# One product's weight tiles moved by 64 bytes within a 512-byte period of SBUF, in an attention and low-rank MLP kernel

## The chip, the cores and the metric

One NeuronCore of a Trainium2 chip runs the whole program. The metric is the device time of one execution in microseconds. A profiled execution has a time of its own, and a span: first to last recorded instruction.

## The reference, cut to what matters

```python
# q, k, v: (8, 8, 576, 64); omega: (128, 64)
q_p, k_p = phi(q * scale), phi(k * scale)     # exp(x @ omega.T - |x|^2/2 - max) / sqrt(128)
attn = (q_p @ (k_p.T @ v)) / (q_p @ k_p.sum(axis=2) + 1e-6)
x = attn.transpose(0, 2, 1, 3).reshape(8, 576, 512)
u = x + (x.transpose(0, 2, 1) @ U @ V).transpose(0, 2, 1)
out = u + np.maximum(u @ w_ch1, 0.0) @ w_ch2  # w_ch1: 512 x 2048, w_ch2: 2048 x 512
```

Inputs and output are float32 (the MLP's weights are decoded from 64-bit words). 4608 rows go through the MLP.

## The kernel before

The work has three stages in order of time. The attention with the mixing by `U` and `V` takes the first 323 us. Then `u @ w_ch1` and the ReLU run until about 690 us, and the product with `w_ch2` runs to the end. The change touches the second and the third stage.

The 4608 rows are cut into 9 chunks `c` of 512 rows, the 2048 columns of `w_ch1` into 4 groups `g` of 512. A block product is done as seven half-size products (Strassen-like sums, `PRODUCTS = 7`), numbered `i`. A float32 number is split into a high and a low part of type float32r, so every product is made of three matmuls: high by high, low by high, high by low.

**Second stage, `unit(c, g, ...)`.** For each of the seven products there are 2 x 2 x 3 = 12 matmuls in L996. Each loads 128 x 128 of a weight tile (`wh` or `wl`, the operand that is held) and streams 256 columns of the right side's tile (`uh` or `ul`, the operand that moves):

```python
for x, y in ((wh, uh), (wl, uh), (wh, ul)):
    K(nc.tensor.matmul(p[:, f, :], x[:, k, fs], y[:, k, :], ...))
```

A chunk from chunk 2 on is 4 groups x 7 products x 12 = 336 matmuls. The order on TensorE is the order of the program (`K` keeps it).

**Third stage, L1379.** 36 steps `n` of 7 products of 12 matmuls. Here the weights of `w_ch2` are the operand that moves, and the left side (`gh`, `gl`; in step 0 also `uT`, `uraw` and `gs`) is held. The weights of group 0 are used in the even steps alone, 6 matmuls for each product.

**Where the weights lie.** `w_slot(g, i)` gives the pair `wh`, `wl` of group `g` and product `i`, 2048 bytes each in a partition. Groups 0 and 1 are in pool `wa`, which is filled from low addresses upward. Groups 2 and 3 are in pool `wb` at the other end. The third stage calls `w_slot` again, so the `w_ch2` tiles take the same places. Several pads in the kernel (`shift`, `rim`) set where the pools start. In the built program the addresses modulo 512 bytes are these:

| tiles | bytes modulo 512 |
|---|---|
| all `wh`, `wl` of groups 0 to 3 | 448 |
| `uh`, `ul` (right side of chunks 0 and 2 to 8) | 128 |
| right side of chunk 1 (it lies in the `wh3`, `wl3` places) | 448 |
| `gh`, `gl`, `gs` (left side of the third stage) | 256 |
| `uT`, `uraw` (left side of the first products of step 0) | 448 |

So moving address less held address, in 64-byte lines modulo 8, is (128 - 448)/64 = 3 for nearly all of the second stage, (448 - 256)/64 = 3 for nearly all of the third, and 0 for chunk 1 and the start of step 0. This text calls it the distance.

Chunks 0 and 1 are interleaved by groups at first, which ends at about 413 us. Chunk 2 runs from there to 452.4 us, and the six chunks 3 to 8 from 452.4 to 689.8 us.

Of the kernel before, what the change touches and what calls it, by code (L numbers as in the profile page):

```python
# [9 lines left out]
F32 = mybir.dt.float32  # L10
F32R = mybir.dt.float32r
# [18 lines left out]
def performer_mlp_kernel(ctx: ExitStack, tc, q, k, v, omega, U, V, w1, w2, out):  # L30
# [12 lines left out]
    P = 128  # L43
# [36 lines left out]
    wpools = {g: wa for g in range(EARLY_GROUPS)}  # L80
# [137 lines left out]

    def w_slot(g, i):
        i = (i - 2) % 7 if g == NG - 1 else i  # L220
        return [wpools[g].tile([P, 2, 2 * P], F32R, name=f"w{a}{g}_{i}") for a in "hl"]

    def operand(g, i):
        if (g, i) not in wops:
            if g == NG - 1 and i < 2:
                if not spares:
                    room = late["rx"].tile([P, 2, PIECE, 2], U32, name="graw0").bitcast(F32R)
                    spares.extend(room.rearrange("p s (k t) w -> p (s k) (t w)", k=2)[:, j] for j in range(4))
                wops[g, i] = [x.rearrange("p (k t) -> p k t", k=2) for x in spares[2 * i : 2 * i + 2]]
            else:  # L230
                wops[g, i] = w_slot(g, i)
        return wops[g, i]
# [823 lines left out]
    def w_place(g):  # L1056
        return lambda i: w_slot(g, i)
# [5 lines left out]
    tp = aside.enter_context(tc.tile_pool(name="tp", bufs=1))  # L1063
    guest_raws = loads(1, tp)
    guest = prepare(1, next(guest_raws), place=lambda i: w_slot(NG - 1, i + 2), lows=(VE, G_) * 3 + (VE,), pool=tp)
    for n, _ in enumerate(mixers[0]):
        if n == 2:
# [166 lines left out]
    for n in range(2, len(order)):  # L1234
        c, g = order[n]
# [123 lines left out]
    for n in range(NS):  # L1359
# [9 lines left out]
        for i in range(PRODUCTS):  # L1369
# [4 lines left out]
            for k in range(4):  # L1374
                g, f = divmod(now.s * 4 + k, 2)
# [70 lines left out]
```

## Time and profile before

| | |
|---|---|
| three runs | 1042.4, 1042.58 and 1048.74 us, median 1042.58 us |
| the profiled execution | 1039.76 us, span 1037.9 us |
| granted TensorE clock, mean over the span | 0.99 |
| TensorE busy, matmul and weight load | 1016.7 and 994.7 us |
| VectorE, ScalarE, GpSimd busy | 849.3, 612.7 and 518.2 us |

A matmul's record begins when the matmul starts and lasts some 0.28 us, though the next one starts after about 0.11 to 0.12 us: records overlap. The pace of the engine is thus read from the distance between starts (the spacing), or from the number of matmuls in a stretch. A stretch counts every matmul that overlaps it, so the spacing is (length + 0.28 us) / count.

### The profile page before, as it was taken

How to read it: one execution, taken by the hardware profiler on the slowest of the kernel's cores; microseconds unless marked ns; L12 is line 12 of the kernel's file. 1: busy time of each engine (PE TensorE's matmuls, PEld its weight loads, DVE VectorE, ACT ScalarE, POOL GpSimd, SP SyncE). 2: the span in 40 equal slices, each digit the busy share in tenths (PEclk: the TensorE clock that was granted, in tenths of full speed). 3: DMA queues.
4: the chain of work that ended last, by engine and by line, in shares of the span. 5: the costliest groups of instructions: out<-in, count | busy, mean ns of one | idle time of the engine just before them, and what ended most of it. 6: DMA issues, size and time to landing. Idle time of an engine off the chain costs nothing.

```text
span 1037.9 us, 23872 instructions
## 1 busy us (share of the span) xinstructions
PE 1016.7 (98%) x8497; PEld 994.7 (96%) x8497; DVE 849.3 (82%) x1510; ACT 612.7 (59%) x1479; POOL 518.2 (50%) x453
## 2 busy tenths in 40 slices
PE   8999999999999989999999999999999999999998
PEld 7998999989988889999999999999999999999998
DVE  4798898998898787666557665779999999999995
ACT  5889899989874556545364453763534444444442
POOL 3446967776433543323405214446575755646543
PEclk9899999999998999999999999999999999999999
DMA  7788687685435775987678767874545555455451
GB/s 136 138 159 155 139 194 142 128 193 121 95 82 126 208 186 123 238 240 193 183 190 222 196 176 246 243 218 158 184 172 183 174 162 176 161 178 178 135 182 51
DMA packets 380630, 175.51 MB, mean 169 GB/s; under 512 B 275680, under 2 KB 353504, under 8 KB 376032
## 3 DMA queue, kind: packets, MB, share of 16 engines
q1 hardware_dynamic: 378144, 173.70, 63.5%
q8 instruction: 67, 1.10, 0.4%
q10 hardware_dynamic: 2368, 0.30, 0.2%
q14 instruction: 51, 0.42, 0.1%
HBM read 109.97 MB, written 63.96 MB: 168 GB/s over the span
## 4 chain that ended last, share of the span: by engine, by line
PE 55%; DVE 2%; DMA 1%; issue 1%; ACT 1%; POOL 0%; SPq 0%; DVEq 0%; ACTq 0%
PE p_p L1379 9%; PE p_q L1379 8%; PE p_n L1379 7%; PE p_n L996 7%; PE p_q L996 5%; PE p_p L996 5%; PE p_kv L1379 4%; PE p_kv L996 3%; PE p_m L996 3%; PE p_m L1379 2%; DMA raw<-in_moe_w_ch_dram 1%; DVE g L984 1%; DMA graw<-g 1%; DVE gl L1224 0%; DMA g<-g 0%
## 5 line engine op out<-in xcount | busy, mean ns | idle before, releaser
L770 ACT ACTIVATE e<-p_p,nm 128x128 f32<-128x128 f32 x576 | 166.1, 397 | 23.3 <-DVE nm L763 16.3
L1217 ACT CAST gh<-gs 128x512 fp32r<-128x512 f32 x140 | 86.4, 622 | 153.0 <-DVE gs L1189 93.1
L1189 POOL TENSOR_TENSOR gs<-graw 128x512 f32<-128x512 f32 x70 | 113.6, 1634 | 121.3 <-DMA graw<-g 86.3
L980 ACT ACTIVATE g<-g 128x512 f32<-128x512 f32 x105 | 66.4, 632 | 165.0 <-DVE g L984 100.7
L636 POOL TENSOR_TENSOR xl<-xT,xh 128x384 fp32r<-128x384 f32 x96 | 97.4, 1031 | 97.5 <-ACT xh L632 80.4
L1224 DVE TENSOR_TENSOR gl<-gs,gh 128x512 fp32r<-128x512 f32 x140 | 137.7, 990 | 6.8 <-ACT gh L1217 6.0
L763 DVE TENSOR_REDUCE nm<-p_p 128x4 f32<-128x512 f32 x144 | 98.1, 683 | 27.0 <-PE p_p L757 12.1
L183 POOL TENSOR_TENSOR wf<-wf,low 128x512 int32<-128x512 int32 (+2 forms) x35 | 43.9, 1254 | 139.9 <-ACT g L980 76.7
L755 PE MATMUL p_p<-omh,xh 128*128 128x256 f32 x288 | 93.5, 325 | 3.6 <-ACT e L770 2.6
L1304 POOL TENSOR_TENSOR u<-u,p 128x256 f32<-128x256 f32 x72 | 80.8, 1151 | 25.7 <-DVE u L1304 23.2
L1224 DVE TENSOR_TENSOR gl<-graw,gh 128x512 fp32r<-128x512 f32 x107 | 84.3, 812 | 4.0 <-ACT gh L1217 4.0
L757 PE MATMUL p_p<-omh,xl 128*128 128x256 f32 x288 | 81.7, 284 | 0.6 <-POOL xl L636 0.6
L756 PE MATMUL p_p<-oml,xh 128*128 128x256 f32 x288 | 81.6, 283 | 0.0
L1379 PE MATMUL p_p<-wh,gh 128*128 128x256 f32 x288 | 79.5, 276 | 0.0
L1379 PE MATMUL p_p<-wl,gh 128*128 128x256 f32 x288 | 79.5, 276 | 0.0
L1379 PE MATMUL p_p<-wh,gl 128*128 128x256 f32 x288 | 79.5, 276 | 0.0
L1217 ACT CAST gh<-graw 128x512 fp32r<-128x512 f32 x107 | 63.4, 619 | 25.9 <-PE p_n L1379 5.1
L1379 PE MATMUL p_q<-wh,gl 128*128 128x256 f32 x276 | 76.3, 276 | 0.0
L1379 PE MATMUL p_q<-wh,gh 128*128 128x256 f32 x276 | 76.2, 276 | 0.0
L1379 PE MATMUL p_q<-wl,gh 128*128 128x256 f32 x276 | 76.2, 276 | 0.0
L713 PE MATMUL p_n<-kv,eT 128*128 128x65 f32 x512 | 73.6, 274 | 1.9 <-ACT eT L698 1.1
L713 PEld LDWEIGHTS p_n<-kv,eT 128*128 128x128 f32 x512 | 68.8, 196 | 5.1 <-ACT eT L698 1.4
(271 smaller groups left out, 3984.0 us busy)
## 6 DMA issues: line engine op xcount, KB each, us to landing
g<-g SPq DMA_DIRECT2D x282, 128.0 KB, 2.3
graw<-g SPq DMA_DIRECT2D x35, 1024.0 KB, 5.2
raw<-in_moe_w_ch_dram SPq DMA_DIRECT2D x22, 512.0 KB, 4.7
u_dram<-ut SPq DMA_DIRECT2D x36, 256.0 KB, 2.5
u<-u_dram SPq DMA_DIRECT2D x36, 256.0 KB, 2.6
out_dram<-u SPq DMA_DIRECT2D x36, 256.0 KB, 2.2
kt<-in_k_dram SPq DMA_DIRECT2D x120, 72.0 KB, 2.5
qt<-in_q_dram SPq DMA_DIRECT2D x120, 72.0 KB, 2.5
```

The lines of the kernel that those rows point to most:

```text
L636: nc.gpsimd.tensor_tensor(out=self.xl[-1], in0=self.turned, in1=f32(self.xh[-1]), op=ALU.subtract)
L713: nc.tensor.matmul(pn[:, h, :], eT[:, h, :], kv[:, h, s // 5, :], start=True, stop=True)
L755: nc.tensor.matmul(o, part.xh[g][:, ts], oh, start=True, stop=False)
L756: nc.tensor.matmul(o, part.xh[g][:, ts], ol, start=False, stop=False)
L757: nc.tensor.matmul(o, part.xl[g][:, ts], oh, start=False, stop=True)
L763: nc.vector.tensor_reduce(out=self.nm[:, :n], in_=self.pp[:, :n], axis=AX.X, op=ALU.max, negate=True)
L770: nc.scalar.activation(out=self.e[:, j, :], in_=self.pp[:, j, :], func=AF.Exp, bias=self.nm[:, j : j + 1])
L996: K(nc.tensor.matmul(p[:, f, :], x[:, k, fs], y[:, k, :], start=first, stop=(k == 1 and y is ul), skip_group_check=True,))
L1189: K(engine.tensor_tensor(out=to, in0=self.val[x], in1=self.val[y], op=op))
L1217: K(nc.scalar.copy(out=h, in_=v))
L1224: K(nc.vector.tensor_tensor(out=l, in0=v, in1=f32(h), op=ALU.subtract))
L1379: K(nc.tensor.matmul(acc[bank][:, half, :], x[:, ks], y[:, f, :], start=(now.s == 0 and k == 0 and half == 0 and x is h and y is wh), stop ...
```

## The change

`w_slot` takes, for group 0 and product 1 alone, a pad of 112 floats (448 bytes) ahead of the two tiles and one of 16 floats (64 bytes) behind them.

```diff
     def w_slot(g, i):
         i = (i - 2) % 7 if g == NG - 1 else i
-        return [wpools[g].tile([P, 2, 2 * P], F32R, name=f"w{a}{g}_{i}") for a in "hl"]
+        pool = wpools[g]
+        if (g, i) == (0, 1):
+            pool.tile([P, 112], F32, name="before")
+        tiles = [pool.tile([P, 2, 2 * P], F32R, name=f"w{a}{g}_{i}") for a in "hl"]
+        if (g, i) == (0, 1):
+            pool.tile([P, 16], F32, name="behind")
+        return tiles
```

No instruction reads or writes the pads. The instructions of the built program and their order and waits are the same on every engine. The addresses are not: the two tiles go from 20928 and 22976 to 21376 and 23424, which is 384 modulo 512. Everything that was above them at that end of SBUF goes up by 512 bytes, and so lies as before modulo 512. What grows from the other end (`wb`, `rx`, the mixing's tiles) stays where it was. The distance of product 1 of group 0 becomes (128 - 384)/64 = 4 (modulo 8) in the second stage and (384 - 256)/64 = 2 in the third; in chunk 1 it becomes (448 - 384)/64 = 1.

## Rows read from the trace of the kernel before

**Rows 1.** The page, part 1: busy us (share of the span) and instructions of each engine.
```profile
PE 1016.7 (98%) x8497; PEld 994.7 (96%) x8497; DVE 849.3 (82%) x1510; ACT 612.7 (59%) x1479; POOL 518.2 (50%) x453
```

**Rows 2.** Busy time by stretch, all engines: busy us (instructions), clock, DMA share, GB/s.
```profile
413.00:429.00 16.00, 16.00 (x143) 16.00 (x143) 9.08 (x16) 10.03 (x19) 1.30 (x1) 1.00 0.90 250
429.00:454.00 25.00, 24.89 (x211) 24.68 (x210) 20.95 (x30) 12.70 (x23) 13.67 (x10) 1.00 0.91 237
454.00:689.80 235.80, 235.80 (x2004) 235.80 (x2003) 152.83 (x230) 117.82 (x207) 77.60 (x58) 1.00 0.75 207
...
710.00:1038.00 328.00, 324.49 (x2864) 324.29 (x2862) 309.22 (x431) 143.08 (x251) 186.68 (x138) 1.00 0.48 158
```

**Rows 3.** Stretches of L996: PE and weight-load busy us (instructions), clock, DMA.
```profile
359.00:368.00 9.00, 9.00 (x77) 9.00 (x76) 1.00 0.86 177
...
414.00:428.00 14.00, 14.00 (x126) 14.00 (x125) 1.00 0.89 245
500.00:680.00 180.00, 180.00 (x1530) 180.00 (x1530) 1.00 0.78 214
```

**Rows 4.** A stretch of L1379, the same columns.
```profile
715.00:1000.00 285.00, 285.00 (x2518) 285.00 (x2517) 1.00 0.52 171
```

**Rows 5.** Groups by line in 415 to 428, 454 to 689 and 359 to 368 us.
```profile
L996 PE MATMUL p_kv<-uh,wh 128*128 128x256 f32 x8 | 2.2, 276 | 0.0
...
L996 PE MATMUL p_n<-uh,wh 128*128 128x256 f32 x190 | 53.4, 281 | 0.0
...
L996 PE MATMUL p_n<-wh,wh 128*128 128x256 f32 x16 | 4.5, 283 | 0.0
```

**Rows 6.** Timeline of PE, 429 us: start us, us, instruction.
```profile
429.18 0.28 PE L996 MATMUL p_p<-ul,wh 128*128 128x256 f32 x1
429.29 0.35 PE L996 MATMUL p_n<-uh,wh 128*128 128x256 f32 x1
429.49 0.28 PE L996 MATMUL p_n<-uh,wl 128*128 128x256 f32 x1
429.60 0.28 PE L996 MATMUL p_n<-ul,wh 128*128 128x256 f32 x1
429.72 0.28 PE L996 MATMUL p_n<-uh,wh 128*128 128x256 f32 x1
```

**Rows 7.** Timeline of PE, 699.9 us.
```profile
699.89 0.28 PE L1379 MATMUL p_q<-wl,gh 128*128 128x256 f32 x1
700.18 0.39 PE L1379 MATMUL p_q<-wh,gl 128*128 128x256 f32 x1
...
700.87 0.28 PE L1379 MATMUL p_q<-wl,gh 128*128 128x256 f32 x1
700.98 0.28 PE L1379 MATMUL p_q<-wh,gl 128*128 128x256 f32 x1
```

**Rows 8.** Timeline of PE, 401.3 us: the moving operand changes from chunk 1's to chunk 0's.
```profile
401.34 0.28 PE L996 MATMUL p_n<-wl,wh 128*128 128x256 f32 x1
401.46 0.29 PE L996 MATMUL p_m<-uh,wh 128*128 128x256 f32 x1
401.58 0.28 PE L996 MATMUL p_m<-uh,wl 128*128 128x256 f32 x1
401.70 0.28 PE L996 MATMUL p_m<-ul,wh 128*128 128x256 f32 x1
401.82 0.28 PE L996 MATMUL p_m<-uh,wh 128*128 128x256 f32 x1
```

**Rows 9.** Timeline of PE, 694 us: the held operand changes from `uraw` to `gh`.
```profile
694.00 0.28 PE L1379 MATMUL p_q<-wh,uraw 128*128 128x256 f32 x1
694.12 0.28 PE L1379 MATMUL p_q<-wh,gh 128*128 128x256 f32 x1
...
694.47 0.28 PE L1379 MATMUL p_q<-wh,gh 128*128 128x256 f32 x1
694.59 0.28 PE L1379 MATMUL p_q<-wl,gh 128*128 128x256 f32 x1
```

## The prediction, made before the changed kernel ran

> **What bounds the kernel now.** I read the busy time by engine first, then by stretch, then the spacing of the matmuls.
>
> TensorE is busy for 98% of the span and its weight loads for 96%; no other engine passes 82% [rows 1]. In the stretches it is busy without a gap from 454 to 689.8 us, where VectorE has 153 of 236 us, ScalarE 118, GpSimd 78, and the DMA engines are 75% busy. In the third stage it is busy for 324 of 328 us, with VectorE close behind at 309 [rows 2]. So the time is the number of matmuls times their spacing, plus few stalls, and the change can only act through one of the two. It adds no matmul. What is left is the spacing.
>
> The spacing is not the same everywhere, although the granted clock is 1.00 in all these stretches. From 414 to 428 us it is (14.00 + 0.28) / 126 = 113.3 ns. From 500 to 680 us, with the same instruction, the same shapes and the same distance of 3 lines, it is 180.28 / 1530 = 117.8 ns. From 359 to 368 us, where the right side is chunk 1's and the distance is 0, it is 9.28 / 77 = 120.5 ns [rows 3]. The third stage runs at 285.28 / 2518 = 113.3 ns [rows 4]. The groups by line show the same three paces in the mean length of a record: 276, 281 and 283 ns [rows 5], so a stretch can be sorted by that number at sight.
>
> So at distance 3 there are two paces, and each lasts. 118 holds without a break from the last stall near 431 us to the end of the second stage: 2004 matmuls overlap 454 to 689.8 us, (235.80 + 0.28) / 2004 = 117.8 ns [rows 2]. What changes the pace is a disturbance. At 429.29 us a matmul comes 0.20 us before the next instead of 0.11; behind it the starts are 0.11 and 0.12 apart, and the pace stays at 118 [rows 6]. At 699.89 us a stall of 0.29 us ends a stretch of 118, and behind it the starts are 0.11 apart [rows 7]. From 323 us on the trace has 16 such stalls at distance 3. Seven fell into a 118 stretch, and the pace behind was 113 after two of them. Eight fell into a 113 stretch, and it was 118 after two. One came at the end of a 120 stretch and left 118. A change of distance is a disturbance too. From 0 to 3 by a new moving operand, without a stall, it comes eight times between 368 and 413 us; one is at 401.46 us, where three starts are 0.12 apart and the pace then is 113 [rows 8]. All eight ended at 113. From 0 to 3 by a new held operand it comes once, at 694 us, and the pace behind is 118: 694.00 to 694.59 us is 0.59 us for five starts [rows 9].
>
> **The change part by part.** The pads and the 512 bytes by which the rest of that end of SBUF rises cost nothing: no instruction is added, and every other tile keeps its place modulo 512. Between the two ends of SBUF the distance in absolute bytes changes by 512; the stretch from 500 to 680 us covers weights at both ends (groups 0 and 1, groups 2 and 3) at one pace [rows 3], so that counts for nothing either.
>
> What the change does is to disturb the pace. In chunks 0 and 2 to 8 the distance goes from 3 to 4 when product 1 of group 0 begins, and back 12 matmuls later: eight passes in the second stage. In the third stage it goes from 3 to 2 and back around 6 matmuls in each even step: 18 passes. The trace has no change between 3 and a neighbour with these shapes, so its effect is bounded by the two paces.
>
> *Second stage.* The first pass that matters is in chunk 3, at about 453.8 us. If it leaves the pace at 113, the remaining 2003 matmuls save 117.8 - 113.3 = 4.5 ns each: 2003 x 4.5 = 9.0 us. If not, 0. VectorE, the next engine, would have 153 of 227 us, and the DMA engines would go from 75% to about 78%, so nothing else takes the time back there. Chunk 2 runs at 113 before its own stalls at 429 and 431 us; if its pass at 414 us spoils that, 126 x 4.5 = 0.6 us are lost.
>
> *Third stage.* It starts its long run at 113. If a pass leaves it at 118 for good, nearly all of the 2864 matmuls from 710 us on [rows 2] pay: 2864 x 4.5 = 12.9 us. If the passes do not change the pace, 0.
>
> *The passes themselves.* By the nearest rows each change of distance costs at most what the one at 401.46 us cost: 0.36 us for three starts against 0.34, so 0.02 us [rows 8]. Two for each of 26 passes give 52 x 0.02 = 1.0 us; the low end is 0. The matmuls inside a pass run at an unknown distance, between 113.3 and 120.5 ns by the same rows: (18 x 6 + 8 x 12) x 7.2 ns = 1.5 us at most. Chunk 1's 12 matmuls go from distance 0 to 1 and gain up to 12 x 7.2 = 0.09 us. I take 0.5 us for all of this together, nearer to the low end, since 2 and 4 are neighbours of 3 and not of 0.
>
> *Sum.* If the passes send the pace to 113 in the second stage and leave it there in the third: -9.0 + 0.5 = -8.5 us. The profiled execution would go from 1039.76 to 1031.3 us. The runs' median is 2.8 us above the profiled execution; with the same gain it goes from 1042.58 to **1034.1 us**, 0.8% less. If those 2.8 us are themselves time at 118 that the profiled execution did not have, the passes could take them too: 1031.3 us.
>
> I take this as the likeliest since changes of distance, unlike stalls, gave the same outcome every time that they came in the same way, and that was 113 in eight of nine; and since the second stage offers six passes at which 118 can end, while one success holds for as long as nothing disturbs it.
>
> **The rivals.**
>
> *The address doesn't matter that way* (chance 0.27). A pass leaves the pace as it finds it: both paces also exist at other distances, or a step of one line is too little. For it: five of seven stalls in a 118 stretch changed nothing. Against it: only the addresses tell chunk 1's 120.5 ns from the other chunks' 113.3 [rows 3]. The time stays at 1042.6 us, give or take the 1.5 us of the passes. The Trainium skill ("SBUF — State Buffer", section on the two separate sides) says that on the engine side only the pair of ports that VectorE shares with GpSimd causes contention, and "TensorE: Matmul & The Clock Gate", step 1 of what a matmul does, that loading the next weights does not take read bandwidth from the running matmul. By that rule this rival holds for certain. The trace disagrees: 120.5 against 113.3 ns at the same clock.
>
> *The third stage falls to 118* (0.15). The same disturbance meets a stage that already runs at the better pace: 36 changes of distance in 328 us, each a chance to fall, and one by the held operand did end at 118 [rows 9]. With the second stage as it is, the price is 12.9 + 0.6 + up to 1.5: 1055 us or a little more. The point from which this side decides: a gain of 8.5 us is eaten when 8.5 / 0.0045 = 1890 of the third stage's 2864 matmuls, two thirds, run at 118. Against it: in the third stage the moving operand is what changes, and that kind of change ended at 113 [rows 8].
>
> *Both paces by turns* (0.18). If each pass draws anew with the odds of the stalls (2 of 7 out of 118, 2 of 8 out of 113), a little over half of each stage runs at 113: about -4.8 us in the second, +6.1 in the third, so 1044 us, with 1037 to 1049 as what such draws can give.
>
> **How the numbers follow.** Likeliest case 0.40, at 1034.1 us (its own range 1030.5 to 1037); the rivals 0.27, 0.15 and 0.18. The range from 1030 to 1049 leaves out the case of a slow third stage and little else, so it should hold 8 in 10. One per cent, about what a measurement of this kernel can tell from no change, is 1032.2 and 1053.0 us. The likeliest case reaches the first only where the passes also take the 2.8 us between the profile and the median, which I give somewhat under half of its 0.40: faster 0.18. The slow third stage reaches the second in most of its 0.15: slower 0.12. The rest is 0.70.
>
> **What would show it.** In the profile after, the mean record of the second-stage matmuls from 460 us on should be 276 instead of 281 ns, the count of matmuls in 180 us near 1591 instead of 1530, and the second stage should end some 9 us earlier. The change of pace should stand within a few starts of the first product 1 of group 0 behind the last stall. In the third stage the record should stay at 276 ns except within the passes. A record of 281 ns in both stages, or 281 in the second and 276 in the third as now, would show the forecast wrong; so would a pace that changes at stalls alone.

## The result and the profile after

| | before | after |
|---|---|---|
| median of 22 runs each, us | 1039.01 | 1043.93 |
| lowest and highest, us | 1031.68, 1053.87 | 1039.74, 1049.76 |
| profiled execution, its span, us | 1039.76, 1037.9 | 1044.16, 1042.3 |

The ratio of after to before is 1.0055, 95% interval 1.0029 to 1.0081: slower by half a per cent, where 0.8% faster was forecast. The range held. Ratios here leave out runs more than 1.5% above the lowest of their kernel, which takes away the four slowest of the 22 runs of before and none of after; the medians are of all runs. Over all 22 runs each the means are 1040.4 and 1044.0 us, 0.3% apart. The lists say more than the medians: 9 of the 22 runs of before are below 1037.6 us, and none of after is below 1039.7.

The work is the same, as the busy times on the page of after show (beside [rows 1]):

```profile
PE 1017.0 (98%) x8497; PEld 994.9 (95%) x8497; DVE 848.4 (81%) x1510; ACT 613.5 (59%) x1479; POOL 517.6 (50%) x453
```

Stretches of TensorE in after: from and to, length, busy us (matmuls), granted clock, DMA share, GB/s. They answer to [rows 2 to 4].

```profile
419.00:454.00 35.00, 35.00 (x299) 1.00 0.90 231
464.50:496.00 31.50, 31.50 (x280) 1.00 0.77 195
498.00:536.00 38.00, 38.00 (x325) 1.00 0.72 190
...
577.00:615.00 38.00, 38.00 (x325) 1.00 0.75 194
715.00:1000.00 285.00, 285.00 (x2511) 1.00 0.51 167
```

With (length + 0.28) / count, chunk 2 behind its pass is at 118.0 ns, the stretch from 464.5 us at 113.5, and every later one between two passes at 117.6 to 117.8. The groups by line in 498 to 535 and then in 465 to 496 us show it in the record's length, as in [rows 5]:

```profile
L1002 PE MATMUL p_n<-uh,wh 128*128 128x256 f32 x32 | 9.0, 281 | 0.0
...
L1002 PE MATMUL p_n<-uh,wh 128*128 128x256 f32 x32 | 8.8, 276 | 0.0
```

So the good pace did occur in the second stage of after. The timeline shows what began it and what ended it (start us, us, instruction). It began at a stall, and it ended at the next pass, the 12 matmuls of product 1 of group 0 at distance 4:

```profile
463.11 0.28 PE L1002 MATMUL p_q<-ul,wh 128*128 128x256 f32 x1
463.83 0.38 PE L1002 MATMUL p_kv<-uh,wh 128*128 128x256 f32 x1 [0.45 <-DVE g L990]
...
496.25 0.28 PE L1002 MATMUL p_q<-uh,wh 128*128 128x256 f32 x1
...
496.59 0.28 PE L1002 MATMUL p_q<-uh,wh 128*128 128x256 f32 x1
...
498.03 0.28 PE L1002 MATMUL p_kv<-uh,wh 128*128 128x256 f32 x1
...
498.26 0.28 PE L1002 MATMUL p_kv<-ul,wh 128*128 128x256 f32 x1
```

From 496.25 to 496.59 us three starts take 0.34 us. From 496.59 to 498.03 us the pass takes 1.44 us for its 12, 120 ns each. Behind it the starts are 0.11 and 0.12 apart, and the pace is 118 until the next disturbance. The passes near 418, 457, 496, 536, 576, 615 and 655 us all ran at 120 ns and all left 118: seven of seven, two from 113 and five from 118.

In the third stage the passes go the other way. Their six matmuls at distance 2 take 115 to 122 ns, and the pace behind is 113 after all 17 that come behind 713 us, each of which found 113; only one in step 0, near 701 us, came at 118 and left 118. From 715 to 1000 us the stage does 2511 matmuls, against 2518 in [rows 4].

**Where the time is by stage.** Each number is a difference of two first starts in the timeline, or of the span's end, which is read to 0.1 us; "pass" names the distances inside it, second stage / third stage (3 is none).

| kernel profiled | pass | first stage | second | third |
|---|---|---|---|---|
| before | 3 / 3 | 323.1 | 366.7 | 348.1 |
| after | 4 / 2 | 326.6 | 366.5 | 349.1 |
| second_only | 4 / 3 | 322.1 | 366.9 | 348.3 |
| third_only | 3 / 2 | 327.2 | 367.2 | 349.2 |
| probe_a | several / several | 324.3 | 361.3 | 359.2 |
| probe_b | several / several | 327.4 | 367.2 | 352.2 |
| shift_control | 3 / 3 | 329.9 | 362.4 | 348.3 |
| sign_flipped | 2 / 4 | 321.8 | 360.0 | 350.3 |
| plus_two_lines | 1 / 2 | 324.9 | 357.8 | 351.6 |
| plus_one_line | 2 / 2 | 321.9 | 359.6 | 349.6 |
| two_passes | 2 / 4, twice | 327.4 | 359.0 | 350.9 |
| pair_of_twelve | 2 / 4, 12 long | 325.1 | 358.0 | 351.2 |
| four_lines | 7 / 7 | 327.6 | 356.8 | 362.8 |

The two profiled executions themselves don't show the change's harm: before's was at 118 in nearly all of its second stage [rows 2], so both second stages last 367 us. Their 4.4 us apart are 3.5 in the first stage, which the change doesn't touch, and 1.0 in the third. What the change does had to be found over many runs and other kernels.

### The profile page after: what moved, and what is told of

The parts are those of the page before. It is cut to its first block, busy times and chain, and to the rows that moved or that the text cites. A ratio compares the mean times of both kernels' runs of the same rounds, so it can differ in the third digit from the quotient of the medians.

```text
span 1042.3 us, 23872 instructions
## 1 busy us (share of the span) xinstructions
PE 1017.0 (98%) x8497; PEld 994.9 (95%) x8497; DVE 848.4 (81%) x1510; ACT 613.5 (59%) x1479; POOL 517.6 (50%) x453
## 4 chain that ended last, share of the span: by engine, by line
PE 58%; DVE 2%; DMA 2%; ACT 1%; issue 1%; POOL 0%; SPq 0%; DVEq 0%; ACTq 0%
PE p_p L1385 9%; PE p_q L1385 8%; PE p_n L1002 8%; PE p_n L1385 7%; PE p_p L1002 6%; PE p_q L1002 5%; PE p_kv L1385 4%; PE p_kv L1002 4%; PE p_m L1002 4%; PE p_m L1385 2%; DMA g<-g 1%; DVE g L990 1%; DMA graw<-g 0%; ACT g L986 0%; DVE wl L532 0%
## 5 line engine op out<-in xcount | busy, mean ns | idle before, releaser
L769 DVE TENSOR_REDUCE nm<-p_p 128x4 f32<-128x512 f32 x144 | 98.1, 683 | 28.4 <-PE p_p L763 12.9
```

The costliest lines, as they stand in the source:

```text
L769: nc.vector.tensor_reduce(out=self.nm[:, :n], in_=self.pp[:, :n], axis=AX.X, op=ALU.max, negate=True)
```

## The experiments

None of the edits changes what the kernel computes. Those on one product's place put its pair of tiles in one tile with 512 bytes of slack, `at` floats above the place it had, 16 to a line of 64 bytes; the two stages can then have offsets of their own:

```python
if (g, i) == (0, 1):
    at = 16 * (A3 if w2_sums else A2)   # third stage : second stage
    room = wpools[g].tile([P, 9 * P], F32R, name="room")[:, at : at + 8 * P]
    return [room[:, j * 4 * P : (j + 1) * 4 * P].rearrange("p (k n) -> p k n", k=2)
            for j in range(2)]
```

`A2` and `A3` are the lines by which the tiles lie higher in the second and the third stage. With the held tile `A2` lines up, the distance in the second stage is 3 - `A2` modulo 8; in the third stage, where it is the moving one, 3 + `A3`.

**1. second_only**: A2 = 7, A3 = 0, the change in the second stage alone.

> The two tiles of group 0, product 1 lie 64 bytes lower modulo 512 in the second stage alone; in the third stage they lie as before. Theory A (the pass to distance 4 and back by the held operand always leaves the pace at 118 ns, whatever it was): in the trace, 120 ns inside each pass and 118 behind it until a stall ends it, in chunks 2 to 8; the third stage as in the kernel before, at 113 or 118 as its last stalls left it. Times: no run under about 1038 us, median 1041 to 1046. Theory B (the paces are drawn by stalls alone, and the changed kernel's loss is the luck of its runs, or comes from the third stage): 113 stays 113 through a pass, some runs near 1032 us, median near the kernel before.

Median 1045.55 us of 12 runs (1039.17 to 1062.2); before beside it 1040.30 of 23; ratio 1.0064 (1.0028 to 1.01). TensorE's stretches behind two stalls, and behind a pass:

```profile
433.00:453.00 20.00, 20.00 (x179) 1.00 0.90 227
461.00:492.00 31.00, 31.00 (x276) 1.00 0.78 196
494.00:531.00 37.00, 37.00 (x317) 1.00 0.73 194
```

113.3 ns behind the stalls at 431.6 and 459.3 us, 117.6 behind the pass at 493 us, and so to the end of the stage. The second stage's passes alone thus bring a slowdown as large as that of the change.

**2. third_only**: A2 = 0, A3 = 7.

> The two tiles lie 64 bytes lower modulo 512 in the third stage alone. Theory A: the passes to distance 2 and back by the moving operand cost about 0.05 us per two steps, under 1 us in all, and leave the pace that they find; the second stage is as in the kernel before, at either pace as the stalls left it, so the runs go down to about 1032 to 1034 us again and the median lies within 2 us of the kernel before. Theory C (the loss comes from the third stage): a loss of 4 to 6 us as in the changed kernel, with 118 ns in long stretches of the third stage.

Median 1042.6 us of 12 (1031.65 to 1045.49), ratio 1.0027 (0.9985 to 1.0069), which alone decides nothing, and the median lies 2.3 us above that of before beside it, where within 2 was expected; but 4 of the 12 runs are below 1036.1 us, as with before and unlike after. The profiled execution (1045.49 us) went from 113 to 118 at a stall at 463.5 us and stayed there, as nothing moved it:

```profile
437.50:463.00 25.50, 25.50 (x228) 1.00 0.92 257
465.00:690.00 225.00, 225.00 (x1913) 1.00 0.75 205
715.00:1000.00 285.00, 285.00 (x2511) 1.00 0.51 167
```

The third stage kept 113 behind each pass. Its 2511 is the count of after, so the passes there cost 7 matmuls of 113 ns, 0.8 us.

**3 and 4. probe_a, probe_b**: which distances do it. Several products get steps of their own, by pads between the sorted tiles of pool `wa`:

```diff
+    lines, at = {(0, 0): 7, (0, 4): 7, (1, 1): 7, (0, 2): 1, (0, 6): 2, (1, 3): 6}, 0   # probe_a
+    lines, at = {(0, 0): 7, (0, 4): 7, (1, 1): 7, (0, 2): 5, (0, 6): 4, (1, 3): 3}, 0   # probe_b
+    for by, g, i in sorted((lines.get((g, i), 0), g, i) for g in range(EARLY_GROUPS) for i in range(7)):
+        if by > at:
+            wa.tile([P, 16 * (by - at)], F32, name=f"pad{by}")
+            at = by
+        for a in "hl":
+            wa.tile([P, 2, 4 * P // 2], F32R, name=f"w{a}{g}_{i}")
+    wa.tile([P, 16 * (8 - at)], F32, name="pad8")
```

The three products with 7 go to distance 4, to set 118; behind each comes a test at another distance, seven times in chunks 2 to 8.

> In groups 0 and 1 six products lie off by lines of 64 bytes: products 0 and 4 of group 0 and 1 of group 1 by -1 (distance 4, meant to set 118 ns), and behind each, after one product at distance 3, a test: product 2 of group 0 by +1 (distance 2), product 6 of group 0 by +2 (distance 1), product 3 of group 1 by -2 (distance 5). Theory A: each step to distance 4 is followed by 118 ns in every chunk from 2 on, and each test leaves one and the same pace in all of these chunks; which one is open (chunk 1 ran at 113 ns inside its pass at distance 1 in the changed kernel, so I expect 113 behind distance 1 at least). Theory B: what stands behind a step differs from chunk to chunk.

> As the other probe, with the tests at product 2 of group 0 by -3 (distance 6), product 6 of group 0 by +4 (distance 7) and product 3 of group 1 by +3 (distance 0). Theory A: 118 ns behind each step to distance 4, the same pace behind each test in all chunks; 120 ns inside the pass at distance 0, and 118 behind it, as at 694 us in the kernel before. Theory B: outcomes differ from chunk to chunk.

1046.62 and 1048.52 us, one run each. The step to 4 ran at 120 ns and left 118 in 21 of 21 cases in probe_a. The tests, all entered at 118:

| distance inside | spacing inside | pace behind | cases |
|---|---|---|---|
| 0 | 120 | 118 | 7 of 7 |
| 1 | 118 | 113 | 7 of 7 |
| 2 | about 119, uneven | 113 | 7 of 7 |
| 5 | 118 | 113 | 7 of 7 |
| 6 | about 119, uneven | 113 | 7 of 7 |
| 7 | 118, no sign of a step | 118 | 7 of 7 |

0 is like 4, 1 like 5, 2 like 6, and 7 like the 3 from which the step is made: for these steps of the held operand only the rest by 4 lines, 256 bytes, counts. The same stretch behind the third test, at distance 5 in probe_a and then at 0 in probe_b:

```profile
470.00:491.50 21.50, 21.50 (x193) 1.00 0.83 207
```

```profile
474.00:496.00 22.00, 22.00 (x189) 1.00 0.83 210
```

21.78 / 193 = 112.8 and 22.28 / 189 = 117.9 ns. The exit of the test at distance 2 in probe_a's timeline:

```profile
496.22 0.28 PE L1004 MATMUL p_kv<-ul,wh 128*128 128x256 f32 x1
496.34 0.28 PE L1004 MATMUL p_m<-uh,wh 128*128 128x256 f32 x1
...
497.04 0.28 PE L1004 MATMUL p_m<-uh,wh 128*128 128x256 f32 x1
497.15 0.28 PE L1004 MATMUL p_m<-uh,wl 128*128 128x256 f32 x1
497.26 0.28 PE L1004 MATMUL p_m<-ul,wh 128*128 128x256 f32 x1
```

The step back is at 496.34 us. By 497.04 us the steps are 0.11.

The test at distance 0 can be set beside the rows of before. There the moving operand came from distance 0 to 3 in the second stage, behind 12 matmuls too, and left 113 [rows 8]: eight of eight in before, and 98 of 98 without a stall over all thirteen traces. In probe_b the held operand comes from 0 to 3, ends on the same places modulo 512, and leaves 118.

In the third stage the same pads step the moving operand, 6 matmuls at a time. In probe_a a pass at distance 2 is followed at once by one at distance 5, and behind them the pace is 118 for the next 90 matmuls, in all 16 even steps in which no stall interferes. In probe_b the second of the two lies at distance 7, and the pace behind is 113, in 16 of 16. One such stretch of each:

```profile
755.80:766.00 10.20, 10.20 (x89) 1.00 0.53 161
```

```profile
763.30:773.20 9.90, 9.90 (x90) 1.00 0.59 187
```

10.48 / 89 = 117.8 and 10.18 / 90 = 113.1 ns. So steps of the moving operand can leave 118 too, and probe_a's third stage lasts 359.2 us for it.

**5. shift_control**: the pads stay, 512 bytes in all, but behind group 1, so that no tile changes its place modulo 512.

> All weights of groups 0 and 1 lie as before modulo 512, and everything above them 512 bytes higher, as in the changed kernel: the change without its offset. Theory A: no difference from the kernel before, a ratio whose interval holds 1, runs from about 1031 to 1053 us, and a pace in the second and third stage that changes at stalls alone. Rival (the 512 bytes by which the rest moves cost time): the loss of 4 to 6 us of the changed kernel again.

Median 1039.41 us of 12 (1029.85 to 1048.62), before beside it 1042.64 of 35 (one of them, at 2543.79 us, lies far off), ratio 0.9984 (0.9937 to 1.003). No effect of the 512 bytes alone is to be seen. The profiled execution shows again what a small stall does when no pass follows; TensorE's stretches before and behind it, and its timeline:

```profile
467.50:580.00 112.50, 112.50 (x995) 1.00 0.78 206
581.50:692.00 110.50, 110.50 (x941) 1.00 0.74 210
```

```profile
580.52 0.28 PE L1004 MATMUL p_q<-ul,wh 128*128 128x256 f32 x1
580.64 0.32 PE L1004 MATMUL p_kv<-uh,wh 128*128 128x256 f32 x1
580.79 0.28 PE L1004 MATMUL p_kv<-uh,wl 128*128 128x256 f32 x1
```

One start 0.15 us behind the last, and 113.3 ns become 117.7 for the rest of the stage.

**6. sign_flipped**: the change with its pads exchanged, one line up.

```diff
-            pool.tile([P, 112], F32, name="before")
+            pool.tile([P, 16], F32, name="before")
...
-            pool.tile([P, 16], F32, name="behind")
+            pool.tile([P, 112], F32, name="behind")
```

> The two pads change places, so that the tiles lie 64 bytes higher modulo 512 instead of lower: distance 2 in the pass of the second stage, 4 in that of the third. Theory A (what a pass leaves depends on its distance: 4 leaves 118 ns, 2 leaves 113): the second stage runs at 113 ns behind each pass of product 1 in every chunk from 2 on, except from a stall to the next pass; the third stage keeps 113 ns through its passes. Median 1032 to 1037 us, 3 to 8 us under the kernel before. Rival (any step away from distance 3 costs): slower than before, as the change.

Median 1033.99 us of 12 (1032.14 to 1040.8), ratio 0.997 (0.9937 to 1.0003), an interval that just holds 1. TensorE's stretch of 118 behind a stall, which lasts to the next pass, and the rest of the stage:

```profile
458.60:491.00 32.40, 32.40 (x277) 1.00 0.76 192
496.00:684.00 188.00, 188.00 (x1656) 1.00 0.78 215
```

188.28 / 1656 = 113.7 ns with four passes in it. The third stage has distance 4 here, the one that leaves 118 in the second; it left 113 every time.

**7. plus_two_lines**: A2 = 2, A3 = 7.

> Second stage: the two tiles 128 bytes higher modulo 512 (distance 1). Third stage: 64 bytes lower, as in the changed kernel (distance 2). Theory A: 113 ns behind each pass in the second stage, and in the third the passes at distance 2 bring 118 back to 113 or keep 113, at under 1 us of cost. Median 1032 to 1036 us, no run above about 1042. Rival (the outcome in the second stage hangs on the pace that the pass meets, so that 113 falls to 118): by turns, median near the kernel before.

Median 1035.58 us of 12 (1031.33 to 1041.28), ratio 0.9986 (0.9951 to 1.0021). TensorE behind 461.5 us, to the end of the stage: (220.50 + 0.28) / 1948 = 113.3 ns, with no time lost in the passes.

```profile
461.50:682.00 220.50, 220.50 (x1948) 1.00 0.77 213
```

**8. plus_one_line**: A2 = 1, A3 = 7, the kinder distance in both stages.

> Second stage: the two tiles 64 bytes higher modulo 512 (distance 2). Third stage: 64 bytes lower, as in the changed kernel (distance 2). Theory A: as with two lines, and 12 x 5.5 ns = 0.07 us more for each of 8 passes, since a pass at distance 2 runs at 119 ns and one at distance 1 at 113 where it starts from 113: median 1032 to 1037 us.

Median 1034.34 us, all 12 runs within 1032.03 to 1036.9; ratio 0.9993 (0.9965 to 1.0022), by the runs of before that the ratio keeps; by the medians of all runs 0.992. TensorE's stretches: 118 behind a stall, 113 behind the next pass, and the same in the third stage.

```profile
431.00:453.50 22.50, 22.50 (x193) 1.00 0.91 238
455.00:492.00 37.00, 37.00 (x329) 1.00 0.79 208
...
702.00:709.50 7.50, 7.50 (x66) 1.00 0.21 70
731.00:747.00 16.00, 16.00 (x144) 1.00 0.57 183
```

118.0, 113.3, 117.9 and 113.1 ns. So the distance-2 pass in the third stage, too, can end 118; it doesn't always, as step 0 of after and of third_only shows, where it came at 118 and left 118. Of the versions tried this one has the narrowest list: it does not beat the best run of before (1028.54 us beside it), but none of its runs is above 1037 us, where before has 26 of 35. That it is better than sign_flipped, with its median of 1033.99, is not shown.

**9. two_passes**: one line up for (0, 1) and (1, 4), with the pads of the probes.

> Product 1 of group 0 and product 4 of group 1 lie 64 bytes higher modulo 512 in both stages: two passes at distance 2 in each chunk of the second stage (some 21 us apart at most instead of 38), two of 6 matmuls at distance 4 in each even step of the third. Theory A: 118 ns that a stall leaves in the second stage ends at the next pass, so it lasts half as long on the mean as with one pass; the third stage keeps 113 through its passes. Median 1032 to 1035 us, no slower than the kernel with one pass 64 bytes higher, and clearly under the kernel before. Rival (a pass costs as much as it brings): no better than before.

Median 1036.78 us of 12 (1033.12 to 1043.4), before beside it 1037.63 of 17, ratio 0.9992 (0.9956 to 1.0029). I had expected no more than with one pass, and a time clearly under before. Neither came: the ratio's interval holds 1, and the median is 2.4 us above that of plus_one_line, which was measured beside other runs of before, with a median 5.0 us higher. The profiled execution was at 113 in both stages, and its first stage lasted 327.4 us. The runs at 1041 to 1043 us have no trace, so whether they lost the pace or the first stage stays open.

**10. pair_of_twelve**: one line up for (0, 1) and (1, 1), so that the third stage has a moving step to distance 4 of 12 matmuls, as long as the held one of the second stage.

> Product 1 of groups 0 and 1 lies 64 bytes higher: in the third stage 12 matmuls in a row at distance 4 by the moving operand, instead of the 6 that kept 113 ns with one product. What decides that a pass at distance 4 leaves 118 is either its length (theory L: 12 matmuls settle at 120 ns, as in the second stage, and 118 stands behind) or the operand that steps (theory H: only a step of the held operand leaves 118): by L the third stage runs at 118 ns and the time is near 1044 us, by H at 113 and the time near 1033 us.

1036.1 us, one run. The 12 settle at 120 ns, as in after's second stage, but the pace behind is 113. The timeline around the step back:

```profile
751.80 0.28 PE L1387 MATMUL p_n<-wl,gh 128*128 128x256 f32 x1
...
752.16 0.28 PE L1387 MATMUL p_n<-wl,gh 128*128 128x256 f32 x1
...
752.40 0.28 PE L1387 MATMUL p_n<-wh,gh 128*128 128x256 f32 x1
...
752.74 0.28 PE L1387 MATMUL p_n<-wh,gh 128*128 128x256 f32 x1
```

From 751.80 to 752.16 three take 0.36 us, from 752.40 to 752.74 0.34. It is not the length of the pass that makes the two stages differ. Theory H fits this run, but not as it is worded: in the third stage of probe_a steps of the moving operand left 118.

**11. four_lines**: A2 = A3 = 4, 256 bytes off.

> The two tiles lie 256 bytes off modulo 512 in both stages: distance 7 in the pass of the second stage and in that of the third. Theory P (what counts of the distance is the rest by 4 lines, since distance 4 ran at 120 ns as 0 does, and 6 did what 2 does): no transient at all at the pass, 113 or 118 ns inside and behind it as ahead of it. Rival (the period is 512 bytes): a change of pace or transient starts within the pass.

1049.06 us, one run. TensorE over the second stage, and over the third:

```profile
421.00:690.00 269.00, 269.00 (x2372) 1.00 0.80 219
715.00:1000.00 285.00, 285.00 (x2422) 1.00 0.48 162
```

269.28 / 2372 = 113.5 ns and 285.28 / 2422 = 117.8. Neither pace was touched by a pass: no start shows one. A stall put the third stage at 118, it stayed, and the stage lasts 362.8 us instead of 348.

## Why the prediction was wrong, point by point

*What bounds the kernel, and the two paces: right.* Both stages are matmuls times spacing. 113.3, 117.8 and 120 ns are the lasting paces of the kernels here, and stalls move a stage from one to the other either way. The price of the second stage at 118 was right too: 366.5 to 367.2 us against 356.8 to 360.0 in the table where it ran at 113, and the term was 9.0. So was that of a third stage at 118: 362.8 against 348.1 to 351.6, and the term was 12.9.

*That the passes set the pace: right, and more firmly than I gave it.* In the second stage a pass fixes it: seven of seven in after, 7 of 7 for each test of the probes, but for distance 7, which does nothing. In the third stage the pass in step 0 of after left the pace as it was.

*Which pace they set: wrong, and this is the step that failed.* I took 113 "since changes of distance, unlike stalls, gave the same outcome every time that they came in the same way, and that was 113 in eight of nine". The eight were steps of the moving operand [rows 8]. The second stage's passes are steps of the held one, of which there was a single row, and it showed 118 [rows 9]. I counted the nine as one kind, though the same sentence sorts them by "the same way". The runs showed 118 in its place, and the second stage at 366.5 us instead of the 356.8 that it lasts at 113 throughout (four_lines). Experiments 1, 4 and 10 show that the kind matters: a step to distance 4 and back left 118 each time by the held operand, and 113 each time by the moving one, also with 12 matmuls; and from 0 to 3 the two operands differ in the same way within one stage.

*"2 and 4 are neighbours of 3 and not of 0": wrong.* Near in bytes meant nothing. By the probes 4 does what 0 does, and 7 does what 3 does. Had I read the 120.5 ns of distance 0 [rows 3] as what 4 would cost, the single row [rows 9], which comes from distance 0, would have pointed to 118.

*The sum.* In place of -9.0 us for the second stage stands a loss against what before draws. Before is at 118 or 113 there as its stalls fall: its second stage and those of third_only and shift_control, which have no pass in it either, last 362.4 to 367.2 us. After is held at 118 from the first pass on, but for what a stall gives back until the next one. By medians that is +4.9 us, about half of the 9.0 between the paces, and the best runs, 1031.7 us, are out of reach. For the third stage the 0 held as to the pace: it stayed at 113. The passes cost 0.8 us there by the count (2511 against 2518), and in the second stage 12 x (120.0 - 113.3) = 0.08 us each at most, 0.6 for seven: 1.4 instead of 0.5 us, within the bounds. The range of 1030 to 1049 us held by luck: it was wide enough for the rivals, and the median lies 9.8 us from the likeliest case.

*The rivals.* "The address doesn't matter that way" is refuted by the change against experiments 6 and 8, and by the probes: the same program is left at 118 or 113 by the place of one pair of tiles. The Trainium skill ("SBUF — State Buffer", section on the two separate sides) says that on the engine side only the port pair that VectorE shares with GpSimd causes contention. As the prediction read it, that rule leaves no room for a pace that hangs on addresses; the runs disagree, with 112.8 and 117.9 ns in one stretch of the two probes. What it is that waits, no run shows. "The third stage falls to 118" did not come; its own terms add up to 1056 us and more, not 1055. "Both paces by turns" gave the nearest time, 1044, for the wrong reason: the draws are before's, and the passes ended them.

*The first stage* was not in the forecast, and it made 3.5 of the 4.4 us by which the two profiles differ.

## What to carry to other kernels

Sort stretches by matmul spacing before anything else: two paces at the same clock, 4% apart and each lasting, hide in one busy TensorE. Here evidence on a disturbance counted only for the same operand and the same distance; where one row is of that kind and eight are not, the one decides, and a kernel that repeats the step a few times settles it in one run. Where runs spread by 2%, look at the list: a change that takes away the best or the worst runs moves the median little.

## What the runs showed of the hardware

**A period of 256 bytes, and a pace that lasts.** The spacing of these 128 x 256 matmuls hangs on the distance of held and moving operand modulo 256 bytes (120.0 ns at 0 and 4, and no sign of a step between 3 and 7), and at distance 3 also on what came before: 113.3 and 117.8 ns are both stable for hundreds of us. From distance 4 or 0 a step back to 3 by the held operand left 118 and one by the moving operand 113. Why is open, and the operand is not all that counts: by way of distances 2 and 5 the moving operand left 118 too. The places of the other tiles were not varied, so the bytes that are stepped between could have a part in it.

**The first stage: an idle time, and the clock behind it.** In after, TensorE stood idle for 2.33 us before 81.54 us, and the granted clock then was 0.50, the 1.2 GHz level, until about 88 us. Timeline and stretches of after:

```profile
81.54 1.11 PE L719 MATMUL p_n<-kv,eT 128*128 128x65 f32 x4 [2.33 <-ACT eT L704]
```

```profile
81.00:84.00 3.00, 2.46 (x12) 0.58 0.87 140
84.00:87.00 3.00, 3.00 (x17) 0.50 0.98 222
87.00:90.00 3.00, 3.00 (x24) 0.78 0.55 84
```

Before, ahead of the same matmul and then in the same stretches:

```profile
79.73 0.66 PE L713 MATMUL p_n<-kv,eT 128*128 128x65 f32 x4 [0.67 <-ACT eT L698]
```

```profile
81.00:84.00 3.00, 3.00 (x29) 1.00 0.83 152
84.00:87.00 3.00, 3.00 (x29) 1.00 1.02 204
87.00:90.00 3.00, 3.00 (x30) 1.00 0.71 113
```

53 matmuls against 88 in 9 us. Counted by the same matmul in both traces, after is 0.15 us behind ahead of this idle time, 1.8 us at its end and 4.5 us near 90 us; at the start of the second stage it is 3.5 us. So the idle time itself brings 1.7 us of the lag, and the lower clock 2.7. Over the 22 runs of after, whose pace is held by the passes, the time goes with the mean granted clock (correlation -0.83; 1039.74 us at 0.996, 1049.76 at 0.987); that it is the first stage there too is not shown, as all of them but one have no trace. Why the idle time is longer in some runs was not tried.
